# Strassen w_out product of a fused attention and FFN kernel: 512 tokens a batch in single PSUM banks, the 64 others as one plain tile

## The chip, the core and the metric

The kernel runs on one core of a Trainium2 chip. The metric is the device time of one execution in microseconds; the median of three runs stands for the kernel. TensorE is called PE, VectorE DVE, ScalarE ACT, GpSimd POOL and SyncE SP; SP issues nearly all transfers, each by an instruction in its queue.

## What is computed

Eight batches of 576 tokens and 8 heads of width 64 attend to 32 pack vectors a head, and the result feeds a GELU FFN with d_model 512 and d_ff 2048:

```python
p_packed = sm_attn(p, k, v)
out = sm_attn(q, p_packed, p_packed)          # 8 batches, 8 heads, 576 tokens, 64
x = out.transpose(0, 2, 1, 3).reshape(B * S, H * D)   # 4608 x 512
h = x @ w_in                                   # 512 x 2048
g = 0.5 * h * (1.0 + erf(h / sqrt(2)))
return g @ w_out                               # 2048 x 512
```

## The kernel before

**Units.** Batches are taken in pairs (four pairs, `pr`) and d_ff in quarters of 512 (`f`); a pair and a quarter are a unit u = 4·pr + f, so there are 16 units, 0 to 15. A product in fp32 is three matmuls for each chunk of the contraction, with fp32r high and low parts of both operands: high by high, high by low, low by high.

**Hidden products** (`hidden_steps`, L1649). Per unit 8 products give a block of 128 rows of d_ff by 576 tokens each, as 12 matmuls of 288 columns into a pair of PSUM banks (`wide`). ACT applies GELU (`gelu`): for units 4 to 15 into SBUF blocks `big` a21, a22, a11 and a12 (token rows of the pair's two batches by halves of the quarter, 128 x 2 x 576). The weights of the hidden products are remade per batch by `wps` products (L1564) with another packing of the PE array (64 x 32 weights).

**Output products of pair 0** (units 0 to 3, `output_steps`, `three`, L1711 to L1713) are plain: tiles of 128 tokens by 512 columns, 3 matmuls of 512 columns for each chunk. The two times 64 tokens left over make one more tile (`edge_output`); POOL cuts their operands (L1701 a cast, L1702 a subtraction, on 128 x 64).

**Output products of units 4 to 15** (`mixed_steps`, L1840) are Strassen's form with seven products, `MIXED` = a22, a11, s2, s3, s1, s4, a12, each for two interleaved column sets h = 0, 1. A product has 12 matmuls of 288 columns: 2 chunks q, 3 split terms, and 2 halves of the 576 tokens, since 576 columns need two PSUM banks. PSUM for them is 2 tiles of 2 banks, used in turn (`twos`, `mps`, opened by `two_banks` when pair 0 is done).
- Left operands: POOL makes the sums s1 to s4 (`sums`, L1758, L1763, 4 a unit, 128 x 1152 elements), ACT casts (`splits`, L1789), DVE subtracts for the low part (`low`, L1795; POOL for the last two of unit 15).
- Right operands are made once, in the first four units, and kept in DRAM as `wx`; `load_one` (L1806) loads 7 of 512 KB a unit into 4 slots `wm`, used in turn; a slot is free when both products of its operand are done. For a11, a12 and s4 the operand is a plain half of w_out, which `keep_blocks` stores half by half.
- `evict` adds the result to SBUF blocks `mac` (DVE L1884, 128 x 576; ACT L1878 for the first of a pair). The products a11, s2, s3, s1 of one h accumulate in one PSUM tile, and the next of them waits for the eviction of the one before. In unit 15 a product goes to up to two blocks at once (DVE L1872).
- `results` and `result` add up, transpose back and store a pair; in the last pair `first_turned` and `last_turned` do it through PE transposes (L1958), copies (L1966) and stores (L1972).

**Order.** Every engine's and the DMA issues' order is a table of numbers, `TURNS`, replayed by the class `Order`. Only `keep_warm` (L1620) adds instructions of its own: bf16 matmuls of 256 columns on a zero tile `still`, wherever PE would else be free before the first output product.

Of the kernel before, what the change touches and what calls it, by code (L numbers as in the profile page):

```python
# [10 lines left out]
F32 = mybir.dt.float32  # L11
# [14 lines left out]
NB32 = S // 32  # L26
NT = NB32 // 2
# [27 lines left out]
NM = len(MIXED)  # L55
LAST_LOW = (5, 6)
# [548 lines left out]
def packed_attention_gelu_ffn(ctx: ExitStack, tc: tile.TileContext, q, k, v, p, w_in, w_out, out):  # L605
# [28 lines left out]
    for t in keys_first:  # L634
        nc.gpsimd.memset(t[64:, 4], 0.0)


    X, ROWS = 4 * 2 * S, 4 * S
    BOTH, EITHER = 2 * 4 * FB, 4 * FB
    place = {}  # L640

# [27 lines left out]
    def plan(order):  # L669
# [823 lines left out]
        def keep_blocks(f, i, src, step):  # L1493
# [10 lines left out]
            for name, _ in mine:  # L1504
                fire(mixed_stored[f, MIXED.index(name)])
# [646 lines left out]
```

## Time and profile before

| what | us |
|---|---|
| median of 3 runs (698.34, 700.01, 698.91) | 698.91 |
| the profiled execution | 696.23 |
| its span, first to last instruction | 694.4 |
| PE busy in the span | 686.9 |

The profiled execution is 2.7 us quicker than the median, and 1.8 us of it lie outside the span. The granted clock was 1.000 over the span. In the rows below, a busy share counts an engine's covered time; a matmul's end is modelled, so the pace of a stream is read from start to start and not from the mean of one. In a row of the timeline the first number is the start, the second the time from the first start to the last end of the instructions joined in it, and the bracket the idle time before it with what ended it.

### The profile page before, as it was taken

What the parts mean: (1) busy time and instruction counts of PE and PEld (TensorE: products, weight loads), DVE (VectorE), ACT (ScalarE), POOL (GpSimd) and SP (SyncE); (2) the same over time, 40 slices, a digit from 0 to 9 for tenths busy, and PEclk for the clock granted to TensorE, in tenths of its full rate; (3) what the DMA queues carried; (4) which work ended last, traced back from release to release, by engine and by line L of the source; (5) the groups of instructions that cost most, each with busy time, mean ns of one, the idle gap of its engine ahead of it and who ended that gap; (6) DMA issues with size and microseconds to landing.
All of it is one profiled execution on the core that took longest, in us unless ns stands there. A gap on an engine that the chain in (4) does not pass through costs nothing.

```text
span 694.4 us, 14848 instructions
## 1 busy us (share of the span) xinstructions
PE 686.9 (99%) x6009; PEld 612.6 (88%) x6009; DVE 537.4 (77%) x699; ACT 394.7 (57%) x600; POOL 286.6 (41%) x203
## 2 busy tenths in 40 slices
PE   9999999999999999999999999999999999999997
PEld 7777787887887998899899998998999899899996
DVE  6789878787999848888998647777899844656785
ACT  5787777766556755575574463575546453534331
POOL 4566753485460553142046633133042824114333
PEclk9999999999999999999999999999999999999999
DMA  9987999988866999999434399986813684423445
GB/s 336 324 229 221 250 267 242 222 279 255 275 230 212 298 252 234 229 225 233 155 122 152 113 214 198 223 222 162 219 62 134 187 223 140 156 89 105 120 145 136
DMA packets 196021, 140.43 MB, mean 202 GB/s; under 512 B 149153, under 2 KB 168673, under 8 KB 195953
## 3 DMA queue, kind: packets, MB, share of 16 engines
q1 hardware_dynamic: 193008, 138.31, 73.1%
q10 hardware_dynamic: 2912, 1.11, 0.7%
q8 instruction: 47, 0.77, 0.5%
q14 instruction: 22, 0.17, 0.1%
q0 software_dynamic: 32, 0.07, 0.0%
HBM read 106.95 MB, written 32.51 MB: 201 GB/s over the span
## 4 chain that ended last, share of the span: by engine, by line
PE 92%; DVE 2%; issue 2%; DMA 1%; POOL 1%; ACT 1%; SPq 0%; POOLq 0%; DVEq 0%; ACTq 0%
PE m L1840 37%; PE h L1649 26%; PE o L1711 5%; PE wps L1564 5%; PE o L1713 4%; PE o L1712 4%; PE s L959 2%; PE h L1640 2%; PE o L1620 2%; DMA wraws<-in_moe_w_out_dram 1%; PE pp L1150 1%; PE e1Tm L1063 1%; DVE memory L2056 1%; POOL rounded L1795 1%; POOL memory L1758 0%
## 5 line engine op out<-in xcount | busy, mean ns | idle before, releaser
L1840 PE MATMUL m<-rounded 128*128 128x288 f32 x2016 | 291.2, 298 | 0.0
L1840 PEld LDWEIGHTS m<-rounded 128*128 128x128 f32 x2016 | 274.9, 196 | 16.2 <-issue 6.6
L1649 PE MATMUL h<-a2T,wp 128*128 128x288 f32 x1440 | 209.4, 295 | 0.0
L1649 PEld LDWEIGHTS h<-a2T,wp 128*128 128x128 f32 x1440 | 197.2, 188 | 4.6 <-ACT memory L1533 0.8
L1758 POOL TENSOR_TENSOR memory<-memory 128x1152 f32<-128x1152 f32 x36 | 101.6, 2824 | 143.5 <-ACT memory L1674 92.1
L1795 DVE TENSOR_TENSOR rounded<-memory,rounded 128x1152 fp32r<-128x1152 f32 x82 | 129.7, 1588 | 28.4 <-ACT rounded L1789 28.4
L1884 DVE TENSOR_TENSOR memory<-m,memory 128x576 f32<-128x576 f32 x124 | 92.5, 748 | 58.4 <-PE m L1840 47.9
L1789 ACT CAST rounded<-memory 128x1152 fp32r<-128x1152 f32 x84 | 96.6, 1158 | 62.0 <-POOL memory L1758 33.0
L1674 ACT ACTIVATE memory<-h 128x576 f32<-128x576 f32 x96 | 61.8, 652 | 97.4 <-PE h L1649 96.1
L1763 POOL TENSOR_TENSOR memory<-memory 128x1152 f32<-128x1152 f32 x12 | 33.5, 2790 | 136.8 <-ACT memory L1674 119.6
L1711 PE MATMUL o<-rounded 128*128 128x512 f32 x128 | 53.3, 416 | 0.2 <-DVE memory L2056 0.2
L1713 PE MATMUL o<-rounded 128*128 128x512 f32 x128 | 50.2, 392 | 0.0
L1712 PE MATMUL o<-rounded 128*128 128x512 f32 x128 | 50.1, 391 | 0.0
L1580 DVE TENSOR_TENSOR wp<-wps,wp 128x1024 fp32r<-128x1024 f32 x30 | 36.5, 1220 | 17.0 <-ACT wp L1575 16.6
L1575 ACT CAST wp<-wps 128x1024 fp32r<-128x1024 f32 x30 | 30.3, 1015 | 33.4 <-PE wps L1564 33.4
L1690 DVE TENSOR_TENSOR rounded<-memory,rounded 128x512 fp32r<-128x512 f32 x32 | 28.9, 902 | 12.4 <-ACT rounded L1688 12.3
L868 DVE STREAM_TRANSPOSE memory<-memory 128x1152 f32<-128x1152 f32 x24 | 32.6, 1367 | 5.8 <-DMA memory<-in_k_dram 5.8
L1479 POOL TENSOR_TENSOR memory<-memory 128x512 int32<-128x512 int32 x16 | 21.8, 1362 | 34.8 <-DVE memory L1451 27.7
L1681 ACT ACTIVATE memory<-h 128x576 f32<-128x576 f32 x31 | 20.1, 652 | 26.0 <-PE h L1649 21.3
L1564 PE MATMUL wps<-memory,pp 64*32 64x512 f32 (+1 forms) x544 | 34.4, 574 | 0.0
L1711 PEld LDWEIGHTS o<-rounded 128*128 128x128 f32 x128 | 24.1, 188 | 11.4 <-issue 6.0
L1471 POOL TENSOR_TENSOR memory<-memory 128x512 int32<-128x512 int32 x16 | 22.3, 1400 | 23.5 <-DVE memory L1451 20.3
(162 smaller groups left out, 827.7 us busy)
## 6 DMA issues: line engine op xcount, KB each, us to landing
rounded<-wx SPq DMA_DIRECT2D x84, 512.0 KB, 4.6
memory<-ws SPq DMA_DIRECT2D x24, 512.0 KB, 4.7
wraws<-in_moe_w_out_dram SPq DMA_DIRECT2D x16, 512.0 KB, 5.4
wx<-memory SPq DMA_DIRECT2D x16, 512.0 KB, 4.5
memory<-in_v_dram SPq DMA_DIRECT2D x15, 512.0 KB, 6.5
memory<-in_k_dram SPq DMA_DIRECT2D x48, 144.0 KB, 5.7
memory<-in_q_dram SPq DMA_DIRECT2D x48, 144.0 KB, 5.5
wx<-rounded SPq DMA_DIRECT2D x24, 256.0 KB, 5.2
```

The costliest lines, as they stand in the source:

```text
L1564: nc.tensor.matmul(t[r0:r0 + 32, hh, :m], lhsT=pp[b][rows, hh, r0:r0 + 32], rhs=wi[u, hh][rows, g, cols], start=True, stop=True)
L1580: yield Op(DVE, 1.22, step, lambda: nc.vector.tensor_tensor(lo, x, hi.bitcast(F32), ALU.subtract))
L1649: nc.tensor.matmul(t[:, half, :HALF], lhsT=w[:, wpart, ch, fc], rhs=a2T[b, ch][:, apart, half * HALF:(half + 1) * HALF], start=ch == 0 and ...
L1674: lambda: nc.scalar.activation(x[:, c % 2].rearrange("p (a n) -> p a n", a=2), t[:, :, :HALF], AF.Gelu), table="gelu")
L1711: nc.tensor.matmul(t, lhsT=g[0], rhs=w[:, 0], start=first, stop=False)
L1712: nc.tensor.matmul(t, lhsT=g[0], rhs=w[:, 1], start=False, stop=False)
L1713: nc.tensor.matmul(t, lhsT=g[1], rhs=w[:, 0], start=False, stop=last)
L1758: return Op(POOL, 2.69, 0, lambda: nc.gpsimd.tensor_tensor(of(x), of(y), of(z), op))
L1789: o = op[u, m] = yield Op(ACT, 1.17, 0, lambda o: nc.scalar.copy(o[:, 0], x), [(ops, f"op_{u}_{m}")])
L1795: engine, cost, 0, lambda: on(engine).tensor_tensor(o[:, 1], x, o[:, 0].bitcast(F32), ALU.subtract), port=True)
L1840: nc.tensor.matmul(t[:, half, :HALF], lhsT=x[:, wpart], rhs=o[:, part, q, half * HALF:(half + 1) * HALF], start=first and q == 0 and wpart ...
L1884: yield Op(DVE, 0.75, 0, lambda: nc.vector.tensor_tensor(to(), x, to(), ALU.add))
```

## The change

- Strassen is done on the first 512 tokens of a batch (`MAIN`), so that a product is 6 matmuls of 512 columns in one PSUM bank; four single banks, any that is free, take the place of the 2 pairs, and `two_banks` goes.
- The 64 others of the two batches (`EDGE`) make one 128-token tile a unit: `cut_edges` on POOL makes their split operands from `big` (4 a unit, on 128 x 2 x 64), `edge_rows` computes them as 2 plain products of 6 matmuls of 512 columns through `three`, and adds them to an SBUF block `edge` (ACT first, DVE after), stored once a pair by two transfers.
- a11, a12 and s4 now read the plain split w_out blocks k0 to k3 (scratch `ws_f_2` to `ws_f_5`, stored whole), which the edge products read too. That makes 8 loads of 512 KB a unit in the same 4 slots, no longer strictly in turn. k0 and k1 are held until a11 and the first edge product are done, k2 and k3 until s4, a12 and the second.
- Operations on 1152 elements shrink to 1024, those on 576 to 512. At the end the stores and transposes of the 64-token pieces go, in the last pair one of the stores on POOL's queue with them. `still` is 128 x 128 and read twice, so the filler matmul keeps its 256 columns; `mx2` has 2 parts instead of 3, and the mixed weights of the first units have a slot of their own.
- All tables of `TURNS` are made anew.

```diff
+MAIN = 512
+EDGE = S - MAIN
+MADE = ("a22", "s2", "s3", "s1")
+LOADS = ("a22", "k0", "s2", "s3", "s1", "k2", "k3", "k1")
+PLAIN = {"a11": (0, 0), "a12": (1, 0), "s4": (1, 256)}
...
-        mps = of_banks([(2 * i, 2 * i + 2, lambda i=i: twos[i]) for i in range(2)], [P, 2, 512], (None, (0, 1)), rank=1)
+        mps = of_banks((None, (0, 1, 2, 3)), rank=1, free=True)
...
-        ops = slots("op", [P, 2, 2, S], F32R, (None, (0, 1, 2)), rank=1)
-        wms = slots("wm", [P, 2, FB], F32R, (None, (0, 1, 2, 3)), rank=1)
+        ops = slots("op", [P, 2, 2, MAIN], F32R, (None, (0, 1, 2)), rank=1)
+        e4s = slots("e4", [P, 2, 2, P], F32R, (None, (0, 1)), rank=1)
+        edges = slots("edge", [P, DM], F32, (None, (0,)), rank=1)
+        wms = slots("wm", [P, 2, FB], F32R, (None, (0, 1, 2, 3)), rank=1, free=True)
...
+        def cut_edges(u, k):
+            e = None
+            for j in range(2):
+                name = f"a{2 - j}{k + 1}"
+                yield value[u, name]
+                if j == 0:
+                    e = e4[u, k] = yield Op(POOL, 0, 0, lambda t: None, [(e4s, f"e4_{u}_{k}")])
+
+                def fn(x=big[u, name], dst=e[:, :, :, EDGE * j:EDGE * j + EDGE]):
+                    x = x[:, :, MAIN:]
+                    nc.gpsimd.tensor_copy(dst[:, 0], x)
+                    nc.gpsimd.tensor_tensor(dst[:, 1], x, dst[:, 0].bitcast(F32), ALU.subtract)
...
+        def edge_rows(u):
+            pr, f = divmod(u, NF)
+            for k in range(2):
+                yield edge_cut[u, k]
+                for q in range(2):
+                    yield wm_ready[u, f"k{2 * k + q}"]
+
+                def product(t, k=k, e=e4[u, k]):
+                    for q in range(2):
+                        three(t, (e[:, 0, q], e[:, 1, q]), wm[u, f"k{2 * k + q}"], q == 0, q == 1)
...
+                fire(halves_done[u, k])
...
+                    a = edge_acc[pr]
+                    yield Op(DVE, 0.685, 0, lambda: nc.vector.tensor_tensor(a, t, a, ALU.add))
...
+        def load_one(u, x):
+            f, plainly = u % NF, x[0] == "k"
+            yield stored[f, 2 + int(x[1])] if plainly else mixed_stored[f, x]
...
+            if plainly:
+                give_when(halves_done[u, int(x[1]) // 2], wms, wm[u, x])
...
                                 for wpart, parts in ((0, (0, 1)), (1, (0,))):
                                     for part in parts:
-                                        for half in halves:
-                                            nc.tensor.matmul(
-                                                t[:, half, :HALF], lhsT=x[:, wpart],
-                                                rhs=o[:, part, q, half * HALF:(half + 1) * HALF],
...
+                                        nc.tensor.matmul(
+                                            t[:, cols], lhsT=x[:, wpart], rhs=o[:, part, q, cols],
...
-                    wms.give(w)
+                    if half is None:
+                        wms.give(wm[u, name])
+                    else:
+                        fire(halves_done[u, half])
```

PE in the last unit, from the last hidden product to s1. Before, a row of L1840 is one product of one h (`m_0` and `m_1` are the pairs of banks): s2 of h = 1, then s3 and s1 of both:

```order
L1649 MATMUL h_127_7357<-a2T_7_0_6010,wp_15_1_6845 128x288 x6
L1649 MATMUL h_127_7357<-a2T_7_1_6110,wp_15_1_6845 128x288 x6
L1840 MATMUL m_1_2677<-rounded_86 128x288 x12
L1840 MATMUL m_0_2676<-rounded_86 128x288 x12
L1840 MATMUL m_1_2677<-rounded_86 128x288 x12
L1840 MATMUL m_0_2676<-rounded_86 128x288 x12
L1840 MATMUL m_1_2677<-rounded_86 128x288 x12
```

The same products after; `o_2` and `o_0` are single banks, and the first two rows are the end of the first edge product:

```order
L1711 MATMUL o_1_88<-rounded_86 128x512
L1712 MATMUL o_1_88<-rounded_86 128x512
L1899 MATMUL o_2_89<-rounded_86 128x512 x6
L1899 MATMUL o_0_87<-rounded_86 128x512 x6
L1899 MATMUL o_2_89<-rounded_86 128x512 x6
L1899 MATMUL o_0_87<-rounded_86 128x512 x6
L1899 MATMUL o_2_89<-rounded_86 128x512 x6
```

A product is 6 matmuls instead of 12, the last hidden product stands further ahead, and an edge product is what now comes before s2 of h = 1; between two products of one h there is one other product in both orders.

SP's queue, the loads of the last unit's weights. Before, one row is a load for one operand, in the order of `MIXED` (L1948 stores results of pair 2):

```order
L1806 DMA rounded_86<-wx_3_0_117 128x1024
L1948 DMA out_0_dram<-memory_83 32x18x64 x4
L1806 DMA rounded_86<-wx_3_1_118 128x1024
L1806 DMA rounded_86<-wx_3_2_119 128x1024
L1806 DMA rounded_86<-wx_3_3_120 128x1024
L1806 DMA rounded_86<-wx_3_4_121 128x1024
L1806 DMA rounded_86<-wx_3_5_122 128x1024
L1806 DMA rounded_86<-wx_3_6_123 128x1024
```

After (`ws_3_2` to `ws_3_5` are k0 to k3, L1834 stores the edge rows of a pair):

```order
L1863 DMA rounded_86<-wx_3_a22_108 128x1024
L1863 DMA rounded_86<-ws_3_2_2097 128x1024
L1863 DMA rounded_86<-ws_3_3_2142 128x1024
L1863 DMA rounded_86<-wx_3_s2_109 128x1024
L1863 DMA rounded_86<-wx_3_s3_110 128x1024
L1863 DMA rounded_86<-wx_3_s1_111 128x1024
L1863 DMA rounded_86<-ws_3_4_2367 128x1024
L1863 DMA rounded_86<-ws_3_5_2399 128x1024
L1834 DMA out_0_dram<-memory_83 64x512 x2
```

There are eight loads where there were seven, two for a11 instead of one, and two (k2, k3) that s4 and a12 share.

PE at the start, from the second hidden product to the first output products, before (L1620 is the filler on `still`):

```order
L1640 MATMUL h_1_786<-memory_83,wp_0_0_606 128x288 x4
L1620 LDWEIGHTS still_72
L1620 MATMUL o_1_88<-still_72 128x256
L1620 LDWEIGHTS still_72
L1620 MATMUL o_1_88<-still_72 128x256
L1640 MATMUL h_2_803<-memory_83,wp_0_0_606 128x288 x4
L1711 MATMUL o_1_88<-rounded_86 128x512
L1712 MATMUL o_1_88<-rounded_86 128x512
L1713 MATMUL o_1_88<-rounded_86 128x512
```

And after, from the first hidden product (L973 are attention scores, L1559 the `wps` products):

```order
L1639 MATMUL h_0_752<-memory_83,wp_0_0_565 128x288 x4
L973 MATMUL o_3_90<-memory_83,pp_1_697 32x288 x4
L973 MATMUL o_0_87<-memory_83,pp_1_697 32x288 x4
L1639 MATMUL h_1_771<-memory_83,wp_0_0_565 128x288 x4
L1710 MATMUL o_1_88<-rounded_86 128x512
L1711 MATMUL o_1_88<-rounded_86 128x512
L1712 MATMUL o_1_88<-rounded_86 128x512
L1559 MATMUL wps_0_1_0_793<-memory_83,pp_1_697 32x256 x8
L1559 MATMUL wps_0_1_1_807<-memory_83,pp_1_697 32x256 x8
```

The fillers between the first hidden product and the first output product are gone, and scores of a later step and `wps` products stand in that stretch.

## Rows read from the trace of the kernel before

**Rows 1.** The page: busy time by engine, and granted clock in 40 slices.
```profile
PE 686.9 (99%) x6009; PEld 612.6 (88%) x6009; DVE 537.4 (77%) x699; ACT 394.7 (57%) x600; POOL 286.6 (41%) x203
...
PEclk9999999999999999999999999999999999999999
```

**Rows 2.** Busy time by stretch of the span, with clock and DMA share.
```profile
core 0: us, PE busy (x) PEld busy (x) DVE busy (x) ACT busy (x) POOL busy (x), PEclk, DMA share, GB/s
232.00:660.00 428.00, 428.00 (x3841) 402.02 (x3840) 319.85 (x370) 226.17 (x309) 150.85 (x55) 1.00 0.69 177
660.00:688.00 28.00, 28.00 (x213) 27.84 (x213) 22.05 (x29) 7.64 (x9) 11.28 (x4) 1.00 0.47 128
```

**Rows 3.** The page, costliest groups: the Strassen matmuls.
```profile
L1840 PE MATMUL m<-rounded 128*128 128x288 f32 x2016 | 291.2, 298 | 0.0
```

**Rows 4.** The chain that ended last: start, duration, what, count (eight products in a row).
```profile
654.65 12.74 PE m L1840 x96
```

**Rows 5.** Timeline, PE, plain output products amid a packed stream.
```profile
179.31 0.39 PE L1711 MATMUL o<-rounded 128*128 128x512 f32 x1
...
184.75 0.95 PE L1649 MATMUL h<-a2T,wp 128*128 128x288 f32 x6
```

**Rows 6.** Timeline, PE, plain output products right after another kind of product.
```profile
154.09 0.40 PE L1712 MATMUL o<-rounded 128*128 128x512 f32 x1
...
156.41 0.39 PE L1713 MATMUL o<-rounded 128*128 128x512 f32 x1
```

**Rows 7.** Chain and timeline, PE: `wps` products in a pair, and one alone.
```profile
208.07 1.88 PE wps L1564 x32
...
260.85 1.09 PE L1564 MATMUL wps<-memory,pp 64*32 64x512 f32 x16
261.87 3.44 PE L1840 MATMUL m<-rounded 128*128 128x288 f32 x24
```

**Rows 8.** Timeline, all engines, the last 9 us.
```profile
685.89 0.38 PE L1958 MATMUL turned_edge<-ident,memory 128*64 128x128 f32 x2
...
689.27 0.69 DVE L1966 COPY memory<-turned_c 128x512 f32<-128x512 f32 x1 [0.53 <-PE turned_c L1958]
...
690.04 0.76 POOL L1972 DMA_DIRECT2D out_dram<-memory  x1 [7.24 <-ACT memory L1966]
```

**Rows 9.** Timeline around the first Strassen product (unit 4, a22).
```profile
230.14 3.79 PE L1840 MATMUL m<-rounded 128*128 128x288 f32 x24
233.77 1.72 PE L1649 MATMUL h<-a2T,wp 128*128 128x288 f32 x12
...
230.72 0.84 PEld L1840 LDWEIGHTS m<-rounded 128*128 128x128 f32 x6 [0.27 <-DVE rounded L1795]
```

**Rows 10.** Groups by form: the fillers before the first output product.
```profile
L1620 PE MATMUL o<-still 128*128 128x256 bf16 x150 | 21.2, 290 | 1.4 <-DVE still L630 1.1 <-ACT memory L886 0.4
```

**Rows 11.** Timeline, last unit, s2 to s1: evictions and PE's weight loads.
```profile
675.41 1.42 DVE L1872 TENSOR_TENSOR memory<-memory,m 128x576 f32<-128x576 f32 x2 [0.84 <-PE m L1840]
...
676.90 1.25 PEld L1840 LDWEIGHTS m<-rounded 128*128 128x128 f32 x9 [0.16 <-issue]
```

**Rows 12.** DMA issues, median us to landing: 232 to 660, 280 to 335, 577 to 676.
```profile
rounded<-wx SPq DMA_DIRECT2D x77, 512.0 KB, 4.7
...
rounded<-wx SPq DMA_DIRECT2D x10, 512.0 KB, 6.4
...
rounded<-wx SPq DMA_DIRECT2D x20, 512.0 KB, 3.3
```

**Rows 13.** Waits of PE's weight loads, 232 to 688: total, times, longest.
```profile
PEld m L1840 <- DVE memory L1884: 6.0, 9, 0.8
```

**Rows 14.** Groups by form: operand work on DVE and the 64-token cuts on POOL.
```profile
L1795 DVE TENSOR_TENSOR rounded<-memory,rounded 128x1152 fp32r<-128x1152 f32 x82 | 129.7, 1588 | 28.4 <-ACT rounded L1789 28.4
...
L1701 POOL CAST rounded<-memory 128x64 fp32r<-128x64 f32 x32 | 13.1, 409 | 12.6 <-ACT memory L1681 12.6
L1702 POOL TENSOR_TENSOR rounded<-memory,rounded 128x64 fp32r<-128x64 f32 x32 | 12.9, 402 | 2.6
```

More of the change, by code (lines that the diff above doesn't have):

```diff
@@ L1619, in keep_warm @@
                     t = r.next("idle")
-                    nc.tensor.matmul(bank(t)[:, :256], lhsT=still[:, :P], rhs=still, start=True, stop=True)
+                    nc.tensor.matmul(
+                        bank(t)[:, :256].rearrange("p (a n) -> p a n", a=2), lhsT=still,
+                        rhs=still.unsqueeze(1).broadcast_to([P, 2, P]), start=True, stop=True)
                     return True
@@ L1757, in put, with free @@
             def put(x, y, z, op):
-                return Op(POOL, 2.69, 0, lambda: nc.gpsimd.tensor_tensor(of(x), of(y), of(z), op))
+                return Op(POOL, 2.4, 0, lambda: nc.gpsimd.tensor_tensor(of(x), of(y), of(z), op))
+            def free(x, name):
+                yield done(name)
+                if (u, x) in cut:
+                    yield cut[u, x]
+                bigs.give(big[u, x])
+            for name, x in (("a22", "a22"), ("s3", "a21"), ("s1", "s1"), ("s4", "a11"), ("a12", "a12")):
+                start(free(x, name))
             yield value[u, "a21"]
@@ L1787, in splits @@
                 yield value[u, name]
-                x = big[u, where.get(name, name)]
-                o = op[u, m] = yield Op(ACT, 1.17, 0, lambda o: nc.scalar.copy(o[:, 0], x), [(ops, f"op_{u}_{m}")])
+                x = main_of(big[u, where.get(name, name)])
+                o = op[u, m] = yield Op(ACT, 1.04, 0, lambda o: nc.scalar.copy(o[:, 0], x), [(ops, f"op_{u}_{m}")])
                 start(low(u, m, o, x))
         def low(u, m, o, x):
-            engine, cost = (POOL, 2.69) if u == NU - 1 and m in LAST_LOW else (DVE, 1.35)
+            engine, cost = (POOL, 2.4) if u == NU - 1 and m in LAST_LOW else (DVE, 1.2)
             yield Op(
@@ L1877, in evict @@
                 mac[pr, name] = yield from one(macs, f"mac_{pr}_{name}", ACT, 0)
[L1878 removed]
+                yield Op(ACT, 0.59, 0, lambda: nc.scalar.copy(to(), x))
             else:
@@ L1893, in results @@
         def results(pr):
-            engine, cost = (DVE, 1.35) if pr == NP - 1 else (POOL, 2.67)
+            engine, cost = (DVE, 1.2) if pr == NP - 1 else (POOL, 2.4)
             def of(name):
@@ L1981, in first_turned @@
             yield evicted[NU - 1, MIXED.index(last), 1]
[L1982 removed]
             y = yield Op(DVE, 0, 0, lambda t: None, [(macs, f"res_{pr}_{name}")])
[L1984 to L1986 removed]
+            z = y.rearrange("p h s -> p (h s)")
+            t = yield Op(PE, 0.44, 0, lambda t: turned(t, 0, src, 0), [(wide, f"turned_{name}")])
+            yield Op(PE, 0.44, 0, lambda: turned(t, 1, src, 2))
             copied = Event(2)
@@ L1989, in first_turned @@
             start(rows_out(t, 0, z[:, :512], 0, r0, v, ACT, nc.sync, copied))
-            start(rows_out(t, 1, z[:, 512:1024], 2, r0, v, DVE, nc.scalar, copied))
-            tail = yield Op(PE, 0.22, 0, lambda t: turned(t, 0, src, 4, 1), [(wide, "turned_edge")])
-            copied = Event()
-            give_when(copied, wide, tail)
-            yield from rows_out(tail, 0, e[:, 256 * v:256 * v + 256], 4, r0, v, ACT, nc.sync, copied)
+            yield from rows_out(t, 1, z[:, 512:], 2, r0, v, DVE, nc.scalar, copied)
         def last_turned(pr, j, v, name, last):
@@ L2093, in plan @@
                 if u >= NF and i >= 2:
-                    start((load_mixed, sums, splits, spare)[i - 2](u), ("mixed_w", "sums", "operands", "steps")[i - 2])
+                    if i < 5:
+                        start((load_mixed, sums, splits)[i - 2](u), ("mixed_w", "sums", "operands")[i - 2])
+                    else:
+                        start(edge_rows(u), "edges")
                     continue
@@ L2116, in plan @@
             start(results(pr), "results")
+        for u in later_units:
+            for half in range(2):
+                start(cut_edges(u, half), "edges")
         return order.run()
```

237 lines of the change are left out of this document (112 added, 125 removed), and 213 rows, old and new, of the table TURNS.

## Prediction

> **What bounds the kernel now.** I began with busy time by engine on the page and the table by stretches. PE is busy 686.9 of 694.4 us, DVE 537.4, ACT 394.7, POOL 286.6 [rows 1]; from 232 to 660 and from 660 to 688 PE is covered without a gap, while DVE has 428.00 − 319.85 = 108 us to spare, ACT 202 and POOL 277, and the granted clock is 1.00, the 2.4 GHz level [rows 2]. So from the first Strassen product on the sum of what PE is given sets the end, and an edit counts by what it does to PE's stream, or by a wait long enough to break it. The waits of PE's weight loads add up to a few microseconds (the largest item 6.0 us in 9 waits, [rows 13]), and as PE stays covered they are hidden under the matmul before. The groups come next: the Strassen matmuls are 2016 with a mean of 298 ns [rows 3]. That mean is a modelled length and overlaps the next one, so I take the pace from starts: 96 of them in 12.74 us, or 132.7 ns each for 288 columns [rows 4].
>
> **The products, by pace.** The pace at 512 columns is not in the Strassen part, but in the plain products of pair 0, with the same number format and a weight load each: from 179.31 to 184.75 there are 24 in 5.44 us, 226.7 ns each [rows 5]. From the one form to the other 224 columns cost 94 ns, 0.42 ns a column, which leaves 132.7 − 288 × 0.42 ≈ 12 ns for an instruction whatever its width. The change takes 14 × 12 = 168 matmuls a unit, 168 × 0.1327 = 22.29 us, and puts 14 × 6 + 2 × 6 = 96 there, 96 × 0.2267 = 21.76 us: −0.53 us a unit, **−6.4 us** in 12 units. There is a slower pace in the trace too: 10 intervals from 154.09 to 156.41, 232 ns each, right after another kind of product [rows 6]. With it a unit costs 22.27 us and the gain is 0.2 us. I take 226.7, since the new products stand in a packed stream, as rows 5 do; the upper end is −0.2, the lower −7.6, if the 288-column matmuls go at 133.3 as in single products of 1.60 us for 12.
>
> **Fewer changes of packing.** The `wps` products use the array in other pieces. A pair of them on the path takes 1.88 us for 32 matmuls, 0.94 for 16, one alone 261.87 − 260.85 = 1.02 for 16 [rows 7], so a change there and back costs about 0.08 us, and about 0.1 with what the next product loses. Counting changes in the two orders of PE from the first output product on gives 84 before and 78 after: **−0.6**, between −1.2 and 0.
>
> **The tail.** The transposes of the 64-token pieces go (two here, two later at the end; 0.22 us on PE from start to start, rows of 0.38 us covered time, [rows 8]), and with them the store on POOL's queue, issued at 690.04, after the last copy of 689.27. The other last store is issued at about the same time, so that only the earlier transposes count: **−0.3**, between −0.6 and 0.
>
> **The first Strassen product.** It waited for DVE: its 24 matmuls took 233.77 − 230.14 = 3.63 us where 24 × 0.1327 = 3.18 was due, and the weight load at 230.72 shows the wait for the low part [rows 9]. After, a hidden product more (12 × 0.13 = 1.6 us) and a `wps` product less (0.93) stand ahead of it, and the subtraction is shorter by a ninth. That closes the gap: **−0.4**, between −0.45 and +0.3 if what makes the operand comes later too.
>
> **The start.** Until the first output product PE runs 150 fillers in 21.2 us, 0.14 each [rows 10]; they are there because PE has no work, so what counts is when the operands arrive. The order after has 4 fillers more overall, none of them between the first hidden and the first output product, where two other steps now stand behind the first hidden product. 4 × 0.14 gives **+0.5**. This is the term that I know least of: the order of all engines is remade there, and with 21.2 us of idle work in it 3 us either way can't be excluded.
>
> **The last unit's chain.** s2, s3 and s1 of one h accumulate in one tile, and the next waits for the eviction of the last, with one product of the other h between. Before, the two evictions took 1.42 us against a product of 12 × 0.133 = 1.60, and PE's weight load waited 0.16 us [rows 11]; so the whole step takes 1.76. After, the evictions shrink by a ninth, 1.76 − 0.16 = 1.60, and the product between to 6 × 0.227 = 1.36: short by 0.24 a step, **+0.3** with what had been lost already, between 0 and +0.8. In units 4 to 14 one eviction is half of that and there is slack.
>
> **The weight loads.** There are 8 a unit instead of 7 in the same 4 slots, and k0 to k3 are held until the edge product too. So a load is issued later before its use. Going through both orders I added up the PE work between the instruction that frees a slot and the first use of what is loaded into it: before it is never under 9.6 us, after it is 8 us or less for 21 of 92 loads, the shortest 4.1, 4.3, 4.3, 5.5 and 5.9. A load of 512 KB lands in 4.7 us in the median, 3.3 in a quiet stretch and 6.4 in a crowded one [rows 12]. The shortest stand in units 15 and 8, in quiet stretches, where 3.3 plus some 0.3 for the signals fits into 4.1. Loads with 5.9 to 6.4 us stand in units 5 to 7, 10 and 11, where the transfers of the next pair crowd the queues: some of them are late by 0 to 0.8 us. I take **+1.0**, from 0 to 4. What is queued behind a load that waits for its slot on SP (the next loads, and stores of results) comes later by the same, and only the next product waits for it.
>
> **Costed at nothing.** DVE's and ACT's operations shrink by a ninth (a subtraction takes 1588 ns now, [rows 14]), and two edge additions of some 0.7 us a unit come on; DVE has 108 us of slack in 428. POOL gets 4 cuts a unit, each twice the size of those of 409 + 402 ns [rows 14], about 1.0 us with half of the cost fixed, or 1.6 if it all scales: 4 to 6.5 us a unit beside 36 us of PE time, against which the four sums shrink by 0.3 each. POOL has 277 us free of 428, so its cover holds, unless a cut stands in the queue ahead of a sum that the next product needs; that is 1 to 1.6 us at such a place, and the order puts the cuts behind the sums that are due. Dropping the bank pairs and the wait at the pool's switch costs nothing visible in the trace.
>
> **The sum** against the profiled execution: −6.4 − 0.6 − 0.3 − 0.4 + 0.5 + 0.3 + 1.0 = **−5.9 us**: the span goes from 694.4 to 688.5, the execution from 696.23 to 690.3. The median stands 2.7 us above that execution, which I keep: 698.9 − 5.9 = **693.0 us**. With its terms' ends the forecast's own range is 690 to 696.
>
> **Rivals.**
> 1. *The wide matmuls go at 232 ns* [rows 6]: the products gain 0.2 instead of 6.4, the sum is +0.3, and the time 699.2, no change. Against it: those ten come right after products with other weights and little work each, while the 24 in a row at 226.7 ns [rows 5] stand in a stream like the new one. Chance 0.08.
> 2. *The weights come late at every unit*: if loads land in 6.4 us + 0.3 not only in crowded stretches but everywhere, the 21 short loads miss by 0.3 to 2.6 us, some 12 us in all, and 693.0 − 1.0 + 12 = 704 us, slower. It decides from a landing of about 6.0 us at each unit on; the extra 6.3 MB and the bunched issue speak for it, the 20 loads at 3.3 us in the last units against it [rows 12]. Chance 0.07.
> 3. *Only columns cost*: if the 12 ns a matmul were not saved with the instruction, a unit would go from 168 × 288 = 48384 to 96 × 512 = 49152 columns, 768 × 0.443 ns = +0.34 us, +4.1 in 12 units, with the rest of the sum +0.5: 703.5, slower. The Trainium skill, page "TensorE: Matmul & The Clock Gate", section "Back-to-back issue gap", comes close to it: N / 2.4 GHz plus some 2.5 ns, by my estimate 122.5 ns at 288 and 215.8 at 512 columns, 20.58 us a unit before and 20.72 after, +1.7 in all, and 698.9 + 1.7 + 0.5 = 701.1. The trace does not agree: 132.7 and 226.7 ns [rows 4, 5]. Chance 0.03.
> 4. *The start comes out quicker* by 3 us, since the fillers between hidden and output product are gone: 689.5. Chance 0.08; the other way, 696.5, is 0.06, still faster.
>
> **How the numbers follow.** The forecast (690 to 696) has 0.68. With rival 4 both ways, 0.82 for faster by over 0.2% (1.4 us, about what a measurement of this kernel can tell from no change); rival 1 makes 0.08 for the same; rivals 2 and 3 make 0.10 for slower. The range of 688.5 to 698.0 takes in the forecast, and rival 4 both ways for the most part, with the loads late by 4 us as its upper end, and leaves out the other rivals.
>
> **What would show it.** In the profile after: 512-column products of L1899 in a packed stream with starts 226 to 228 ns apart confirm the main term, 232 refutes it. Weight loads of PE that wait for DMA at L1899 or L1710, above 0.5 us each, would be the late weights, first at s1 and k1 of units 7, 8 and 15. A first output product earlier or later than in the trace before by more than 1 us would be the start. POOL among the releasers of ACT's casts more than now would be a cut in a bad place. If PE is no longer covered from 232 to 660, my claim that nothing but PE counts there is wrong.

## The result and the profile after

The changed kernel takes 702.35 us (median of 6 runs, 701.18 to 703.87) beside 698.87 us for the kernel before: 1.0061 of it, 95% interval 1.0042 to 1.0080. So it is slower, by 3.5 us in the median, where 5.9 us less was forecast. The profiled execution has a span of 700.3 us against 694.4; 2.4 of these 5.9 us come from the profiled execution of the kernel before, which was a quick one (696.23 us, 2.6 under the median), while that of the changed kernel took 702.12. A second measurement, beside its own runs of the kernel before, gave 1.0090 (1.0061 to 1.0119).

The page of the changed kernel, answering [rows 1] and [rows 3] (busy time by engine; the Strassen matmuls, now at L1899, with count, busy time and mean):

```profile
PE 688.3 (98%) x5151; PEld 563.7 (80%) x5151; DVE 524.6 (75%) x720; ACT 383.9 (55%) x601; POOL 318.1 (45%) x298
L1899 PE MATMUL o<-rounded 128*128 128x512 f32 (+1 forms) x1014 | 260.0, 396 | 3.4 <-DVE memory L2101 1.5
```

PE still fills the span, with half the Strassen instructions. But it is no longer without gaps from 232 to 660, as the table by stretches shows (the same columns as [rows 2]):

```profile
232.00:660.00 428.00, 424.51 (x3041) 352.64 (x3041) 303.63 (x383) 216.81 (x310) 177.40 (x143) 1.00 0.73 189
660.00:690.00 30.00, 29.98 (x140) 24.85 (x139) 26.38 (x33) 7.52 (x8) 15.48 (x13) 1.00 0.36 121
```

From 232 to 660 PE was not covered for 3.5 us. The greater part of the miss is the pace, which covered time doesn't show. The timeline of PE in units 14 and 15, where nothing waits (start, covered time, count):

```profile
663.14 2.96 PE L1899 MATMUL o<-rounded 128*128 128x512 f32 x12
665.94 0.39 PE L1710 MATMUL o<-rounded 128*128 128x512 f32 x1
...
667.31 2.96 PE L1899 MATMUL o<-rounded 128*128 128x512 f32 x12
```

Twelve Strassen matmuls take 665.94 − 663.14 = 2.80 us, 233 ns each; the six of the edge product that follows take 1.37 us, 228 ns each. Number format, width and clock are the same. The prediction had taken the 226.7 of [rows 5] for all of them.

The waits of PE's weight loads from 232 to 690 (total, times, longest), answering [rows 13], show two new items:

```profile
PEld o L1899 <- DMA rounded<-ws: 2.0, 2, 1.9
PEld o L1899 <- DVE memory L2101: 2.0, 1, 2.0
```

The second is the start of unit 4 (timeline, answering [rows 9]): the second product of a22 goes to bank `o_0`, and the addition that empties it (L2101) stands on DVE behind a subtraction for the mixed weights (L1531), which ran 2.88 us:

```profile
230.68 2.88 DVE L1531 TENSOR_TENSOR memory<-memory 128x512 fp32r<-128x512 f32 x1
...
231.12 1.56 PE L1899 MATMUL o<-rounded 128*128 128x512 f32 x6
...
233.48 0.68 DVE L2101 TENSOR_TENSOR memory<-o,memory 128x512 f32<-128x512 f32 x1
...
234.21 1.66 PE L1899 MATMUL o<-rounded 128*128 128x512 f32 x6 [1.53 <-DVE memory L2101]
```

The first is k3 of unit 5. On SP's queue and on PE:

```profile
292.06 1.56 PE L1899 MATMUL o<-rounded 128*128 128x512 f32 x6
293.55 1.20 PE L973 MATMUL s<-memory,pT 64*32 64x288 f32 x32
...
292.28 4.77 SPq L860 DMA_DIRECT2D memory<-in_q_dram  x4
297.15 1.94 SPq L1863 DMA_DIRECT2D rounded<-ws  x1
...
303.05 0.97 PE L1899 MATMUL o<-rounded 128*128 128x512 f32 x3 [1.43 <-DMA rounded<-ws]
```

The slot of that load was free when s3 of the unit (first row) ended, at 293.5 us. The load was issued at 297.15, behind four transfers of the next pair's queries, and landed at 303.0, with PE waiting.

At the end, answering [rows 8], the last copy and the last store:

```profile
694.45 0.69 DVE L2024 COPY memory<-turned_c 128x512 f32<-128x512 f32 x1 [0.53 <-PE turned_c L2017]
695.17 0.39 ACTq L2030 DMA_DIRECT2D out_dram<-memory  x1
```

From the start of the last copy to the end of the span it was 694.4 − 689.27 = 5.1 us before, and is 700.3 − 694.45 = 5.9 us now.

### The profile page after: what moved, and what is told of

Read it like the earlier page. It is cut to its first block, busy times and chain, and to the rows that moved or that the text cites. A ratio compares the mean times of both kernels' runs of the same rounds, so it can differ in the third digit from the quotient of the medians.

```text
span 700.3 us, 13274 instructions
## 1 busy us (share of the span) xinstructions
PE 688.3 (98%) x5151; PEld 563.7 (80%) x5151; DVE 524.6 (75%) x720; ACT 383.9 (55%) x601; POOL 318.1 (45%) x298
## 4 chain that ended last, share of the span: by engine, by line
PE 84%; DMA 7%; DVE 4%; ACT 2%; issue 2%; SPq 0%; ACTq 0%; DVEq 0%
PE o L1899 33%; PE h L1648 24%; PE o L1710 5%; PE o L1712 4%; PE o L1711 4%; PE wps L1559 4%; PE s L973 2%; DMA wraws<-in_moe_w_in_dram 2%; DMA wraws<-in_moe_w_out_dram 2%; PE o L1617 1%; DMA p<-in_p_dram 1%; DMA rounded<-wx_s 1%; PE pp L1164 1%; DMA wf<-memory 1%; PE e1Tm L1077 1%
## 5 line engine op out<-in xcount | busy, mean ns | idle before, releaser
L1899 PE MATMUL o<-rounded 128*128 128x512 f32 (+1 forms) x1014 | 260.0, 396 | 3.4 <-DVE memory L2101 1.5
L1899 PEld LDWEIGHTS o<-rounded 128*128 128x128 f32 x1014 | 188.0, 194 | 49.7 <-issue 7.8
L1850 DVE TENSOR_TENSOR rounded<-memory,rounded 128x1024 fp32r<-128x1024 f32 x82 | 116.9, 1432 | 37.1 <-ACT rounded L1844 37.0
L1760 POOL TENSOR_TENSOR memory<-memory 128x1024 f32<-128x1024 f32 x36 | 89.4, 2483 | 83.2 <-DVE rounded L1850 47.6
L1844 ACT CAST rounded<-memory 128x1024 fp32r<-128x1024 f32 x84 | 88.1, 1051 | 63.9 <-PE o L1899 49.2
L1944 DVE TENSOR_TENSOR memory<-o,memory 128x512 f32<-128x512 f32 x124 | 83.3, 680 | 51.1 <-PE o L1899 51.0
L1673 ACT ACTIVATE memory<-h 128x576 f32<-128x576 f32 x96 | 62.0, 652 | 102.3 <-PE h L1648 96.7
L1773 POOL TENSOR_TENSOR memory<-memory 128x1024 f32<-128x1024 f32 x12 | 31.5, 2622 | 125.9 <-ACT memory L1673 107.1
L1710 PE MATMUL o<-rounded 128*128 128x512 f32 x176 | 72.5, 412 | 0.1
L1712 PE MATMUL o<-rounded 128*128 128x512 f32 x176 | 69.0, 392 | 0.0
L1711 PE MATMUL o<-rounded 128*128 128x512 f32 x176 | 68.6, 390 | 0.0
L1710 PEld LDWEIGHTS o<-rounded 128*128 128x128 f32 x176 | 33.0, 188 | 16.2 <-issue 8.9
L1797 POOL CAST rounded<-memory 128x128 fp32r<-128x128 f32 x48 | 26.2, 546 | 37.9 <-ACT memory L1673 22.3
L1712 PEld LDWEIGHTS o<-rounded 128*128 128x128 f32 x176 | 33.0, 188 | 7.4
L1711 PEld LDWEIGHTS o<-rounded 128*128 128x128 f32 x176 | 33.1, 188 | 5.5
L1488 POOL TENSOR_TENSOR memory<-memory 128x512 int32<-128x512 int32 x16 | 23.0, 1439 | 25.6 <-DVE memory L1460 20.2
L1559 PE MATMUL wps<-memory,pp 64*32 64x512 f32 (+1 forms) x544 | 34.0, 573 | 0.0
```

Of the source, the lines that this page charges most:

```text
L1559: nc.tensor.matmul(t[r0:r0 + 32, hh, :m], lhsT=pp[b][rows, hh, r0:r0 + 32], rhs=wi[u, hh][rows, g, cols], start=True, stop=True)
L1673: lambda: nc.scalar.activation(x[:, c % 2].rearrange("p (a n) -> p a n", a=2), t[:, :, :HALF], AF.Gelu), table="gelu")
L1710: nc.tensor.matmul(t, lhsT=g[0], rhs=w[:, 0], start=first, stop=False)
L1711: nc.tensor.matmul(t, lhsT=g[0], rhs=w[:, 1], start=False, stop=False)
L1712: nc.tensor.matmul(t, lhsT=g[1], rhs=w[:, 0], start=False, stop=last)
L1760: return Op(POOL, 2.4, 0, lambda: nc.gpsimd.tensor_tensor(of(x), of(y), of(z), op))
```

## Experiments

The theory from these rows: the Strassen matmuls read their weight tile with a stride of two columns (`x0 + h` with a step of 2, since h picks the even or odd columns), the plain ones read 128 adjacent columns, and the stride is what costs 6.5 ns (233.3 − 226.7). The rival: the wide matmul of this part costs 233 ns whatever the layout. Beside it stood the wait in unit 4 and the late weights.

**Adjacent columns in the changed kernel.** The w_out blocks are written with even columns first and odd ones after in each 256, and the results are put back in order when they leave PSUM:

```diff
-                                x0 = (q * 256 if half is None else c0) + h
-                                x = w[:, :, x0:x0 + 256 - h:2]
+                                x0 = (q * 256 if half is None else c0) + h * P
+                                x = w[:, :, x0:x0 + P]
...
-                    lambda: nc.gpsimd.tensor_tensor(d[:, 1], full.bitcast(F32), d[:, 0].bitcast(F32), ALU.subtract))
+                    lambda: nc.gpsimd.tensor_tensor(
+                        kept(d[:, 1]), read(full.bitcast(F32)), kept(d[:, 0].bitcast(F32)), ALU.subtract))
```

> The changed kernel, with the columns of w_out kept apart by parity (even ones first, odd ones after, within each 256), so that the stationary operand of a Strassen product is 128 adjacent columns instead of every second one; the sums go back to the natural order where they leave PSUM. Nothing else moves. Theory stride: the Strassen matmuls go at 233 ns instead of 227 because their weights are read with a stride of two; here they go at 226 to 227 as the edge products do, 1008 x 6.5 ns = 6.5 us less, 702.35 - 6.5 = 695.9. Rival width: 512 columns in this part cost 233 ns whatever the weights' layout (moving operand, PSUM bank); then 233 stays and the time is 702 to 703. Price for both: the reordering reads on ACT, DVE and POOL may cost up to 1 us in the first 230 us.

Measured: 700.28 us, 1.0019 (1.0002 to 1.0036) of the kernel before. The timeline of PE at the same place as above:

```profile
664.00 2.88 PE L1906 MATMUL o<-rounded 128*128 128x512 f32 x12
666.72 0.39 PE L1717 MATMUL o<-rounded 128*128 128x512 f32 x1
```

2.72 us for twelve, 226.7 ns each. The stride it is, for the pace. Of the 6.5 us some 3 reach the time (1.0061 to 1.0019). The profiled execution, at 702.23 us the slowest of the twelve, shows loads late at 424 and 426 us, and after them the granted clock at its lower level (last section).

**A stride in the plain products.** The other direction:

```diff
-                        cols = slice(i * P, (i + 1) * P)
+                        at = i // 2 * 256 + i % 2
+                        cols = slice(at, at + 255, 2)
```

> The changed kernel, with the plain output products of units 0 to 3 taking every second token of 256 as a weight tile instead of 128 adjacent ones (the tokens of pair 0 come out in another order); their 64-token tile and the edge products of units 4 to 15 stay adjacent. Theory stride: the plain products of units 0 to 3 go at 233 ns instead of 227 in a packed stream, 384 x 6.5 ns = up to 2.5 us more where PE is the bound, the edge products stay at 227. Rival width: the plain products stay at 227.

Measured: 703.52 us in a single run, too little to see up to 2.5 us in the time. In the timeline of PE, twelve plain matmuls in a packed stream of unit 3:

```profile
200.19 0.40 PE L1710 MATMUL o<-rounded 128*128 128x512 f32 x1
...
202.75 0.40 PE L1712 MATMUL o<-rounded 128*128 128x512 f32 x1
```

Eleven intervals in 2.56 us, 233 ns each. A stride of two makes a plain matmul as slow as a Strassen one.

**Adjacent columns in the kernel before.** The same edit on 288-column products.

> The kernel before with the same columns kept apart by parity, so that its 288-column Strassen matmuls read adjacent weights. Theory stride: starts are 132 ns apart instead of 133 (as the hidden products with adjacent weights), at most 2016 x 1 ns = 2 us less, 697 to 699; a stride costs less at 288 columns than at 512. If a strided weight load cost 6 ns at any width it would be 12 us less, 687. Rival width: no change, 698.9.

Measured: 699.58 us, 1.0011 (0.9987 to 1.0035): no difference. The median start to start of the Strassen matmuls went from 133 to 132 ns. At 288 columns the stride is nearly free, so a pace taken from the Strassen matmuls of the kernel before could not have shown it either.

The weight loads could have. Their rows in the kernel before, Strassen products first and hidden products second, then the Strassen products of this run, of the changed kernel and of the changed kernel with adjacent columns (the second number after the bar is the mean of one in ns):

```profile
L1840 PEld LDWEIGHTS m<-rounded 128*128 128x128 f32 x2016 | 274.9, 196 | 16.2 <-issue 6.6
L1649 PEld LDWEIGHTS h<-a2T,wp 128*128 128x128 f32 x1440 | 197.2, 188 | 4.6 <-ACT memory L1533 0.8
...
L1847 PEld LDWEIGHTS m<-rounded 128*128 128x128 f32 x2016 | 272.6, 188 | 17.6 <-DVE memory L1891 7.4
L1899 PEld LDWEIGHTS o<-rounded 128*128 128x128 f32 x1014 | 188.0, 194 | 49.7 <-issue 7.8
L1906 PEld LDWEIGHTS o<-rounded 128*128 128x128 f32 x1014 | 183.4, 189 | 52.2 <-issue 6.0
```

With the stride a weight load takes 194 to 196 ns, without it 188 or 189. So the page of the kernel before showed that the Strassen products load their weights more slowly than the others; what that does to a 512-column product it did not show.

**The wait in unit 4.** Two places changed in DVE's table: the addition on bank `o_0` goes ahead of the subtraction for the mixed weights.

> The changed kernel with one DVE instruction moved: the last addition of pair 0 on PSUM bank o_0 goes ahead of a subtraction for the mixed weights. In the changed kernel the second Strassen product of unit 4 waits 1.7 us for that bank. Theory: that wait is gone, PE being the bound, and the time is 1.5 us less, 700.8. Rival: the subtraction that moves back, or the next operand, is late instead and the time stays at 702.4.

Measured: 703.65 us over 9 runs (699.84 to 708.40), 1.0082 (1.0051 to 1.0113). The wait, 1.5 us of idle PE and 1.7 us from start to start, is gone: the product of h = 1 follows that of h = 0 without a gap.

```profile
233.49 2.83 PE L1897 MATMUL o<-rounded 128*128 128x512 f32 x11
```

But the time is not less. PE waited 0.9 to 1.4 us for loads at four places of the profiled run, and 1.95 us at 90 us for a GELU. So the wait was there, and what it is worth is not seen in this run.

**The changed kernel again, and with fewer loads.** Four kernels on one chip. The edit that leaves out loads, and with them a part of the weights:

```diff
+            if x in ("k1", "k3"):
+                yield Op(DMA, (1, 524e3), 0, lambda: None)
+                fire(wm_ready[u, x])
+                return
...
-                                w = wm[u, ws[q if len(ws) > 1 else 0]]
+                                w = wm[u, ws[0]]
```

and the rule on free banks and slots:

```diff
-        for x in self.last[1]:
-            if self.clear(x):
-                return x
-        return None
+        clear = [x for x in self.last[1] if self.clear(x)]
+        return min(clear, key=self.since) if clear else None
```

> The changed kernel once more, beside the next three on one chip, as their yardstick: about 0.6% over the kernel before, some 702 us.

> The changed kernel with 6 weight loads a unit instead of 8: k1 and k3 are not loaded, and k0 and k2 are read in their place (this leaves out a part of the weights). PE's instructions and their order stay. With 6 loads in 4 slots a slot is free long before its next use. Theory late weights: the stalls of 0.3 to 1.8 us in units 5 to 10 that move from run to run are loads that come late since k0 to k3 hold their slots; without them 2 to 4 us less than the changed kernel, and the spread of its runs shrinks to that of the kernel before (about 4 us). The 233 ns of the Strassen matmuls and the 1.7 us wait in unit 4 stay. Rival: the stalls come from operands (DVE, POOL) or from the attention work of the next pair; then less than 1 us changes.

> The changed kernel with the weights' columns kept apart by parity (adjacent stationary columns), and with one rule changed: of several free PSUM banks or slots the one that has been free longest is taken, not the one with the lowest number. The second product of unit 4 then takes a bank that was drained long before. Theory: 227 ns a matmul (-5.5 us, of which the runs have shown some 3 in the median) and no 1.7 us wait: 3 to 5 us less than the changed kernel beside it, at the kernel before or up to 1 us under it; what is missing to 7 us is taken back by late weights, which are nearer to their use when PE is faster. Rival: late weights take back all of it, no change against the changed kernel.

> All three together: adjacent stationary columns, the longest-free bank, and 6 loads a unit (k1 and k3 not loaded, k0 and k2 read in their place, which leaves out a part of the weights). Theory: pace, bank and late weights are what separates the forecast of 693.0 from the 702.4 measured; with the three gone the time is 693 to 695, 4 to 5 us under the kernel before. Rival: something else holds 3 us or more (start, tail, the attention work), then 697 or more.

| kernel, beside 697.44 us before | us | of the kernel before (95%) |
|---|---|---|
| changed kernel again | 704.83 | 1.0090 (1.0061 to 1.0119) |
| with 6 loads a unit | 700.63 | 1.0042 (1.0026 to 1.0059) |
| adjacent columns, longest-free bank | 701.08 | 1.0040 (1.0023 to 1.0058) |
| all three | 694.14 | 0.9954 (0.9937 to 0.9970) |

PE in 232 to 660, by stretches, of the changed kernel again, of the one with 6 loads, and of all three:

```profile
232.00:660.00 428.00, 423.12 (x3011) 349.49 (x3010) 303.85 (x383) 215.07 (x308) 174.64 (x139) 1.00 0.73 188
```

```profile
232.00:660.00 428.00, 426.25 (x3055) 354.81 (x3055) 306.61 (x385) 218.01 (x312) 179.91 (x143) 1.00 0.64 165
```

```profile
232.00:660.00 428.00, 427.52 (x3083) 355.31 (x3082) 311.78 (x390) 218.60 (x312) 184.00 (x146) 1.00 0.64 164
```

PE's gaps shrink from 4.9 to 1.75 to 0.5 us, and the runs with 6 loads lie within 2 us of each other (699.23 to 701.16) where those of the changed kernel spread over 7 (700.67 to 708.02). The theory of late weights holds against its rival: without k1 and k3 4.2 us go (the two intervals just don't overlap). The run takes away more than the change had added, though, as the kernel before has 7 loads a unit.

With all three the kernel comes out at 694.14, 10.7 us under the changed one, so these three causes are the greater part of the miss. They are not the whole of it: the forecast was 0.9916 of the kernel before, 691.5 beside these 697.44, and 0.9954 (0.9937 to 0.9970) was measured. 2.6 us are left, and 3.3 us under the kernel before are less than the 4 to 5 expected. A part of what is left is the start: the first Strassen product comes at 232.16 us in this profile, in the kernel before at 230.14.

```profile
232.16 2.22 PE L1915 MATMUL o<-rounded 128*128 128x512 f32 x9
```

With the loads left in, pace and bank together bring 3.75 us, not enough for the time of the kernel before that was expected; with the loads left out they bring 700.63 − 694.14 = 6.5. In the profile with the loads left in PE's weight loads waited 4.7 us for late loads in 5 places, against 3.1 in 2 of the changed kernel again: late loads take back a part of what PE gains. That each load then has less PE work to hide behind is the likely reason. What the bank is worth in time no run shows: 1.0019 with adjacent columns alone and 1.0040 with the longest-free bank too, on two chips, don't differ beyond their intervals.

**Where the late loads come from.** For each load I set beside each other the end of the last product that used its slot, its issue, its landing and its first use. In the changed kernel those with the shortest way from a free slot to the first use were issued 0.2 us after the slot was free and landed in time (s1 of unit 15 with 1.6 us to spare, k1 of unit 8 with 1.3). Those that were late or had under 0.4 us to spare (k3 of units 4, 5 and 8, k1 and s3 of unit 5, s2 of unit 10) were issued 1.3 to 7.4 us after their slot was free, behind other transfers, mostly input loads of the next pair, and took 4.4 to 7.8 us to land. So a new order of SP's queue:

> The changed kernel with SP's queue in another order: 21 of the 96 weight loads of units 4 to 15 go ahead of the input loads of the next pair (q, k, v, p, hidden weights) that stood before them, where the trace shows that their slot was free by then; in the changed kernel the loads that came late (k3 of units 4, 5 and 8, s2 of unit 10) were issued 2 to 12 us after their slot was free, behind those input loads, while the loads of units 8 and 15 with the shortest way from a free slot to their use were issued 0.2 us after it and landed in time. Nothing else moves. Theory queue: the stalls of units 4 to 10 shrink from about 3 us to under 1, 2 to 3.5 us less than the changed kernel, 1.004 of the kernel before, as with 6 loads a unit. Rival slots: the loads are late for want of a free slot, the order of the queue changes less than 1 us, 1.007 to 1.009. Second rival: the input loads that are now later hold up the next pair's attention by as much.

> The whole computation, with the three things that the runs have named put right: adjacent stationary columns (227 ns), the longest-free bank, and the weight loads ahead of the input loads in SP's queue. With a part of the loads left out the same kernel took 0.9954 of the kernel before. Theory queue: 0.996 to 0.998 of the kernel before, 695 to 696.5 beside a 697.5. Rival slots: as without the new order, 1.004, 701.

Measured: 707.05 us, 1.0110 (1.0077 to 1.0144), and 705.96 us, 1.0097 (1.0063 to 1.0131). Both are worse. In the second no weight load was late any more (the shortest had 1.1 us to spare), but the waits of PE's weight loads have a new item, for the transposes of the pack vectors:

```profile
PEld pTm L948 <- issue: 5.1, 1, 5.1
```

The load of the pack vectors of batch 4, issued at 269.7 us without the new order, now stood behind two weight loads, was issued at 274.1 and held PE until 280.8. The second rival of the first run was right. With the p loads left in their places:

> As the run with all three put right (adjacent stationary columns, longest-free bank, weight loads ahead of input loads), but the small loads of the pack vectors (p) of the next batches keep their place in SP's queue, save that k3 of unit 4 still goes ahead of one. In the run before no weight load was late any more, but PE waited 5 us for the pack vectors at 276 us and again near 437, since their loads stood behind weight loads that waited for a slot. Theory queue: both kinds of late loads are gone, 0.996 to 0.999 of the kernel before. Rival: whatever goes ahead delays something else on the one queue, 1.003 or more.

Measured: 698.89 us, 1.0018 (1.0000 to 1.0036). This lies between what theory and rival gave. It is not better than the kernel before, and its interval overlaps that of 1.0040 without a new order (1.0023 to 1.0058), so that a gain isn't shown. Now k1 of unit 5 was 2.1 us late. And with 15 loads issued by ACT:

> The kernel with adjacent stationary columns and the longest-free bank, SP's queue in the order of the changed kernel, but 15 of the 96 weight loads (s3, k3 of unit 4; a22, k0, k1, s3, k3 of unit 5; k0, k1 of 6; k2, k3 of 8; a22, s1 of 9; a22, s2 of 10), those which SP issued 2 to 15 us after their slot was free with under 2.5 us to spare, are issued by ACT at the same place of the program. They pass the input loads without delaying what SP issues. Theory queue: the late weights go (as with a part of the loads left out, where the same kernel took 0.9954), less what the same bytes cost on the shared DMA engines: 0.996 to 0.999 of the kernel before. Rival engines: it is the 16 DMA engines that are full, not SP's queue; then the loads land as late as before, 1.002 to 1.004. Second rival: ACT is held up by its loads, 1.004 or more.

Measured: 709.87 us, 1.0176 (1.0131 to 1.0220), above what the theory and the first rival gave. Most loads from both queues took 6 to 8 us around 250 to 300 us, and PE waited for the next pair's inputs:

```profile
PEld pTm L948 <- DVE wp L1587: 3.0, 1, 3.0
PEld pp L1169 <- DMA memory<-in_v_dram: 2.8, 2, 2.1
```

The loads did not pass without delaying what SP issues. In the waits of SP's queue (232 to 690: total, times, longest) the issues of the next pair's k and q (L865) now wait until weight loads have landed:

```profile
SPq L865 <- DMA rounded<-ws: 15.0, 4, 7.7
SPq L865 <- DMA rounded<-wx_s: 13.8, 3, 8.5
SPq L865 <- DMA rounded<-wx_a: 9.6, 2, 5.1
```

Eight of these nine waits end with the landing of a load that ACT had issued. In the same kernel without ACT's loads no issue of L865 waits for a weight load. Why they wait here the trace doesn't say. So the input loads came late by the edit itself, and the run decides nothing between SP's queue and the DMA engines.

Are the engines full in these stretches? The rows by stretch of the kernel before (first fence), of the changed one (second) and of the one with 6 loads a unit (third; the last but one number is the DMA share):

```profile
232.00:300.00 68.00, 68.00 (x581) 63.42 (x580) 48.99 (x47) 39.14 (x58) 26.50 (x12) 1.00 1.03 252
400.00:450.00 50.00, 50.00 (x424) 46.21 (x423) 31.92 (x33) 25.19 (x35) 14.24 (x5) 1.00 1.04 208
```

```profile
232.00:300.00 68.00, 66.47 (x454) 53.63 (x454) 44.37 (x46) 34.59 (x53) 32.93 (x30) 1.00 1.05 239
400.00:450.00 50.00, 50.00 (x333) 41.33 (x333) 30.39 (x34) 26.59 (x39) 19.41 (x16) 1.00 1.06 224
```

```profile
232.00:300.00 68.00, 66.34 (x455) 53.72 (x455) 45.92 (x45) 35.07 (x54) 33.37 (x29) 1.00 0.95 226
400.00:450.00 50.00, 50.00 (x335) 41.36 (x334) 30.33 (x35) 26.60 (x39) 19.22 (x16) 1.00 0.98 203
```

The share is about 1 in all three, but only the changed kernel had late weight loads there. So a share near 1 doesn't by itself make a load late. That an eighth load finds no room on the engines is a possible account and not shown: leaving out two loads takes away bytes, issues on SP and held slots at once. That a fifth slot would help wasn't tried.

## Why the prediction was wrong

What bounds the kernel was read rightly in the main: PE's sum sets the end, and the changes count by what they do to its stream. By the prediction's own sign, the claim that nothing but PE counts from 232 to 660 failed: PE was uncovered there for 3.5 us, in the second measurement for 4.9. The steps, against the profiled spans (+5.9 us where −5.9 was forecast; +3.5 in the medians); the measured ones add up to +5.3:

- **The products** (forecast −6.4). This is the term that failed most. 12 × (84 × 0.2333 + 12 × 0.2283 − 22.29) = +0.6 us: nothing gained, 7 us off. The failed step is the sentence that took [rows 5] because the new products "stand in a packed stream, as rows 5 do". Number format, width and one weight load each were compared, the pattern in which the weight tile is read was not; the source shows it, as a slice with a step of 2 on the one side and none on the other. The 12 ns an instruction, which the wider products were to save, came from the same mix, a strided pace at 288 columns and an adjacent one at 512. Between the two strided paces, 132.7 and 233.3, it is (233.3 − 132.7) / 224 = 0.449 ns a column, which leaves 3.4 ns. Rival 1 had the pace (232 ns), with 0.08, for another reason; its time, 699.2, is 3 us short. Rival 3 (703.5, with 0.03) lies nearest to the measured time by luck: with adjacent columns the 226.7 that it took for a sign of cost by column alone brought no 703.5, but 700.28. The range held 232 only as a bound.
- **The weight loads** (forecast +1.0, from 0 to 4). In the changed kernel's profile about 2 us, by the run with fewer loads 4.2 us, the forecast's upper end. The step that failed is how it was counted: by the way from a free slot to the first use. That picked units 15 and 8 and the like, which landed in time; the late ones were issued late, behind other transfers on SP's queue, and landed slowly (k3 of unit 5: 3.6 us after its slot was free, 5.9 us to landing). Whether the queue, the engines or the held slots are the root stays open. Rival 2 (704, with 0.07) was right on the sign; its time was near by luck, as it put 12 us on late loads at every unit and left the products at −6.4.
- **The first Strassen product** (forecast −0.4). Its operand did come in time, but the second product waited 1.5 us for a bank, where 0.45 had been lost before: +1.1. In the text PSUM banks were costed at nothing; the order of PE alone doesn't show which bank is emptied last on DVE.
- **The tail** (forecast −0.3): +1.0. From the first of the last matmuls to the last copy 0.25 us more, and 0.7 us more from there to the end. That the last stores now share the engines with others is a guess that no run here tested.
- **The start** (forecast +0.5): the first output product came 3.0 us earlier (46.86 us against 49.86), as rival 4 had it, but the first Strassen product 1.0 us later, with a hidden product more and a `wps` product less (+0.7) ahead of it: +0.3. The work that was moved behind the first output product had to be done all the same. In the profile of the second measurement the first Strassen product comes at 232.54 us, 2.4 us later than before: there PE waited 1.31 us at 89 us for a GELU (L1680) to empty a bank, a wait that neither the kernel before nor the first profile has.
- **The last unit's chain** (forecast +0.3): the wait at s1 is 0.43 us on the weight loader in place of 0.16, as worked out. The changes of packing weren't measured apart.

Of the chances, 0.82 for faster was too much. The main term rested on one pace from another part of the kernel, and the rivals that pointed the other way were held improbable one by one.

## What to carry to other kernels

A matmul's pace may be carried from one part of a kernel to another only if the weight tile's access pattern is the same too; a slice with a step is seen in the source, and a run with adjacent columns settles it. A mean weight load that differs from that of the other groups (196 against 188 ns here) is a sign of it in the trace. Before a change adds transfers, look at what stands ahead of them on the issuing queue: here the added loads were late in the stretches in which the next pair's inputs are loaded, and of the new orders two made the pack vectors late and the third still left a load late. A load's slack is to be counted from when its queue can issue it, not from when its buffer is free.

## What the runs showed of the hardware

A stationary tile read with a stride of two 4-byte columns costs 6.5 ns in a 512-column matmul (226.7 to 233.3, in both directions of the test) and about 1 ns in one of 288 (133 to 132 without it, tested in one direction). The weight loads take 194 to 196 ns with the stride and 188 or 189 without, at both widths.

A late load costs more than its wait. In the second measurement of the changed kernel PE waited 2.10 us for a load of unit 5, and the twelve hidden matmuls that came after the next three took 2.85 us from start to start, where 1.58 is usual. Timeline of PE, and the stretches with PE's clock in the third number from the right:

```profile
306.85 0.99 PE L1899 MATMUL o<-rounded 128*128 128x512 f32 x3 [2.10 <-DMA rounded<-ws]
307.66 3.06 PE L1648 MATMUL h<-a2T,wp 128*128 128x288 f32 x12
310.51 1.81 PE L1899 MATMUL o<-rounded 128*128 128x512 f32 x6
```

```profile
306.00:309.00 3.00, 2.15 (x9) 2.04 (x10) 2.86 (x11) 2.06 (x6) 0.00 (x0) 0.78 0.92 332
309.00:312.00 3.00, 3.00 (x14) 2.75 (x13) 0.05 (x1) 1.21 (x1) 0.00 (x0) 0.65 1.25 278
```

The granted clock fell to 0.78 and 0.65 in these stretches, a mean over the levels of 2.4 and 1.2 GHz, and was back at 1.00 after 312. The same is seen after PE's waits with adjacent columns (0.22 and 1.66 us at 424 and 426 us) and, with the weight loads ahead of the input loads, after the 4.7 us for the pack vectors:

```profile
427.00:430.00 3.00, 3.00 (x9) 2.19 (x7) 2.03 (x3) 0.00 (x0) 0.47 (x2) 0.50 0.91 127
...
283.00:287.00 4.00, 4.00 (x30) 2.68 (x36) 3.03 (x5) 0.44 (x1) 0.00 (x0) 0.59 0.95 356
```

In the first profile of the changed kernel, after a wait of 1.43 us, the clock stayed at 1.00. How much of the spread of the changed kernel's runs comes from the clock isn't shown: of the six runs of the second measurement the slowest (708.02 us) has a mean clock of 0.996, but the two next (706.58 and 706.05) have 0.998 and 0.999.
